# Low halves of h issued one by one, two halves of w2 cast by VectorE, a half of w1 by GpSimd

## The chip, the cores and the metric

One core of one Trainium2 chip. The metric is the device time of one execution in microseconds (us); the time before is the median of three runs, 408.17 us (408.06 to 408.4). The program text calls the engines V (VectorE, DVE in the profile), A (ScalarE, ACT), P (GpSimd, POOL), T (TensorE, PE) and SY (SyncE, SP, which here only issues DMAs).

## The reference

The output is the sum of two branches on inputs of 2048 tokens by 448 channels (the listing leaves out the shapes and the spectral branch's name for its weight):

```python
def _A_ref(x, w_r, w_i):                       # branch A: a filter in the frequency domain
    X = jnp.fft.rfft2(x, axes=(-2, -1)) * (w_r + 1j * w_i)
    return jnp.fft.irfft2(X, s=(S, D), axes=(-2, -1))
def _B_ref(x, w1, w2, w3, w4):                 # branch B
    h = _gelu(_layernorm(x, axis=-1) @ w1)
    # the four quarters of h's channels are moved by +1, -1, +2, -2 tokens -> hs
    x1 = x + hs @ w2
    return x1 + _gelu(_layernorm(x1, axis=-1) @ w3) @ w4
```

The change lies in the first 50 us of branch B, up to the product with w2.

## The kernel before

**Tiles.** The tokens are 16 blocks of 128, in four groups of four (`GRP`); token block b of a group is one half of a tile `xt`. Every product is made with numbers split into two 16-bit halves: a high half (the value rounded to float16) and a low half (value minus high half). So a matrix product takes three passes (high by high, low by high, high by low), 11 matmuls of 128x448 for one block of tokens.

**Stages around the change.** `norm1(g)` takes the layernorm statistics of a group (BN_STATS, BN_AGGR, L306 and L307), a first guess of the inverse root (L324 to L328), and normalises the four blocks in place (L333 on ACT, L336 on DVE or POOL). `powers` (L255) makes a power-of-two scale for a weight matrix from its sum of squares. `split_w` (L274) splits a weight: in the form with `low is P`, POOL scales the source in place (L276), ACT writes the high half (L277) and POOL the low half (L278); in the other form ACT writes the scaled high half (L280) and DVE the low half (L281). The four row tiles of w1 are split at L884, the last two in the POOL form, and the four of w2 at L923, all in the POOL form.

`T1(g)` transposes a normalised group on PE (L389, banks `pta`), ACT writes the high half of the transpose (L393) and DVE the low half (L394). `w1_in` (L420) is the product with w1. `w1_unit(g, i)` finishes block i of group g: gelu on ACT (L459), the high half of h on ACT (L460), and **two** low halves on DVE, one after the other (L462, k = 0 and 1; 224 columns each). The writes place the four quarters of h's channels in four different slots of `x2mem`, which is how the tokens are shifted: k = 0 writes into the slots of the two blocks behind (c-2 and c-1), k = 1 into those of the two blocks ahead (c+1 and c+2). When a block's slot has all its quarters (`DONE`), SP issues a DMA transpose of it into `hT` (L470, `h<-x2mem` in the profile). `w2_tile(b)` (L474) multiplies the block by w2 (11 matmuls L478), and DVE adds the product, scaled, into `xt` (L479).

The tile w2p holds the four high halves (slots 0 to 3) and the low halves (slots 7 to 10); two DMA copies (L924 and L925) put the high halves on the other partitions into slots 3 to 6. `load_w3([3])` and `load_w4(8, 6)` (L223, L238) are loads from HBM that SP issues behind the last DMA transpose of the first group. `turn(3)` (L854) makes the transposes of group 3 by DMA (L863, `xT<-x`), not on PE.

**Order.** A scheduler orders each engine's instructions by priorities in program order. `behind(key)` pins instructions: they are issued after the instruction that is filed under the key in `after` (`("n", 2)`: group 2's last normalisation on DVE, `("na", 2)` that on ACT, `("np", 2)` that on POOL; `("w1", t)`, `("w2", t)`: the split of a tile; `("h", g, i)`: a DMA transpose; `("r1",)`, `("e1",)`: the start and the end of w1's scale on DVE). SP issues DMAs in its order; each queue of an engine works in its order.

Of the kernel before, what the change touches and what calls it, by code (L numbers as in the profile page):

```python
# [15 lines left out]
AF = mybir.ActivationFunctionType  # L16
ALU = mybir.AluOpType
# [108 lines left out]
def body(tc, nc, x, wf, w1, w2, w3, w4, c_g, c_n, c_small, out):  # L126
    V, A, P, T, SY = nc.vector, nc.scalar, nc.gpsimd, nc.tensor, nc.sync
# [28 lines left out]
    def bank(tag, name):  # L156
        return ps.tile([128, 512], F32, tag=tag, bufs=2, name=name)
# [10 lines left out]
    def xb(b):  # L168
        return xt[b // 2][:, b % 2]
# [7 lines left out]
    def stage(name, n, side, dtype=F32):  # L177
        t = pw.tile([128, 1808], F32, tag=f"stage{side}", bufs=1, name=name)
        return (t if dtype is F32 else t.bitcast(dtype))[:, :n]
# [24 lines left out]
    w1s = stage("w1s", F, 0).rearrange("p (t n) -> p t n", t=4)  # L204
    w2s = stage("w2s", F, 1).rearrange("p (t n) -> p t n", t=4)
# [65 lines left out]
    def absmax(out_, in_):  # L271
        V.tensor_reduce(out=out_, in_=in_, axis=AX.X, op=ALU.max, apply_absolute_value=True)

    def split_w(hi, lo, src, s, low=None):  # L274
        if low is P:
            after["ps"] = (P.tensor_scalar(out=src, in0=src, scalar1=s, scalar2=0.0, op0=ALU.mult, op1=ALU.add).ins,)  # L276
            i = A.activation(out=hi, in_=src, func=AF.Copy)  # L277
            j = P.tensor_tensor(out=lo, in0=src, in1=hi, op=ALU.subtract)  # L278
            return i.ins, j.ins
        i = A.activation(out=hi, in_=src, func=AF.Copy, scale=s)  # L280
        j = V.scalar_tensor_tensor(out=lo, in0=src, scalar=s, in1=hi, op0=ALU.mult, op1=ALU.subtract)  # L281
        return i.ins, j.ins

# [35 lines left out]
    def norm1(g, apply, pins=None):  # L319

        bs, c = GRP[g], slice(4 * g, 4 * g + 4)
        mv, a, y, nm = mva[:, c], va[:, :, c], vy[:, :, c], nma[:, c]
        stats([xb(b) for b in bs], f"a{g}", mv, pins)
        V.tensor_scalar(out=a[:, 1], in0=mv[:, :, 1], scalar1=1.0 + EPS, scalar2=EPS * EPS, op0=ALU.mult, op1=ALU.add)  # L324
        V.tensor_scalar(out=a[:, 0], in0=mv[:, :, 1], scalar1=EPS, scalar2=None, op0=ALU.add)
        V.tensor_single_scalar(vyi[:, :, c], va.bitcast(I32)[:, :, c], 1, op=ALU.logical_shift_right)
        V.tensor_scalar(out=vyi[:, :, c], in0=vyi[:, :, c], scalar1=-1, scalar2=0x5F3759DF, op0=ALU.mult, op1=ALU.add)
        i = V.scalar_tensor_tensor(out=nm, in0=mv[:, :, 0], scalar=-1.0, in1=y[:, 1], op0=ALU.mult, op1=ALU.mult)  # L328
        after["c", g] = (i.ins,)
        for k, b in enumerate(bs):  # L330
            y_, m_ = y[:, 1, k:k + 1], nm[:, k:k + 1]
            if apply[k] is A:
                i = A.activation(out=xb(b), in_=xb(b), func=AF.Identity, scale=y_, bias=m_)  # L333
                after["na", g] = (i.ins,)
            else:
                i = apply[k].tensor_scalar(out=xb(b), in0=xb(b), scalar1=y_, scalar2=m_, op0=ALU.mult, op1=ALU.add)  # L336
                after["n" if apply[k] is V else "np", g] = (i.ins,)

        q, z = (pc.tile([128, 2, 4], F32, tag=f"v{t}", bufs=2, name=f"v{t}{g}") for t in "qz")
        w, r = vw[:, :, c], vr[:, :, c]  # L340

        def refine():
            P.tensor_tensor(out=q, in0=y, in1=y, op=ALU.mult)
            P.tensor_tensor(out=q, in0=q, in1=a, op=ALU.mult)
            P.tensor_scalar(out=w, in0=q, scalar1=-10.0 / 3.0, scalar2=None, op0=ALU.add)
            P.tensor_tensor(out=w, in0=w, in1=q, op=ALU.mult)
            P.tensor_scalar(out=w, in0=w, scalar1=5.0, scalar2=None, op0=ALU.add)
            P.tensor_tensor(out=z, in0=w, in1=w, op=ALU.mult)
            P.tensor_tensor(out=z, in0=z, in1=q, op=ALU.mult)
            P.tensor_scalar(out=z, in0=z, scalar1=-0.5 * 0.375 ** 3, scalar2=1.5 * 0.375, op0=ALU.mult, op1=ALU.add)  # L350
            P.tensor_tensor(out=r, in0=z, in1=w, op=ALU.mult)
            i = P.tensor_scalar(out=gsc[:, c], in0=r[:, 1], scalar1=r1, scalar2=None, op0=ALU.mult)
            after["g", g] = (i.ins,)
        return refine
# [17 lines left out]
    after = {}  # L372

    @contextlib.contextmanager
    def behind(*key):
        key = key if len(key) > 1 else key[0]
        with contextlib.ExitStack() as st:
            for i in after[key]:
                st.enter_context(tc.issue_after(i))
            yield  # L380
# [26 lines left out]
    w1p = p1.tile([128, 8, D], F16, name="w1p")  # L407
    w2p = pr.tile([128, 11, D], F16, name="w2p")
# [5 lines left out]
    def w1_in(g, units, ts, passes=range(3)):  # L414
        for p in passes:
            for t in ts:
                for i, pm in units:
                    wi, xi = ((0, 0), (0, 4), (4, 0))[p]
                    if t < 3 or p != 1:
                        m = T.matmul(pm[:, :D], xTs[g][:, xi + t, 128 * i:128 * i + 128], w1p[:, wi + t],  # L420
                                     start=t == 0 and p == 0, stop=t == 3 and p == 2)
        after["u"] = (m.ins,)
# [25 lines left out]
        for b, k in ((-2, slice(224, 448)), (-1, slice(336, 448))):  # L448
            P.tensor_copy(out=slot(b)[:, :, k], in_=slot(b - 2)[:, :, k])

    def w1_unit(g, i, pm=None):
        if pm is None:
            pm = bank(("tr" if g == 1 else "mm", "acc")[i // 2], f"pw1_{g}{i}")
            w1_in(g, [(i, pm)], range(4))
        c = CS[GRP[g][i]]
        pm = pm[:, :D]
        pv_ = pm.rearrange("p (i j n) -> p i j n", i=2, j=2)
        h = [slots_of((GRP[g][i] + 2) % NB - 2, k) for k in range(2)]
        A.activation(out=pm, in_=pm, func=AF.Gelu_apprx_tanh, scale=gsc[:, c:c + 1])  # L459
        u = A.activation(out=h[0], in_=pv_, func=AF.Copy, scale=h1)  # L460
        for k in range(2):
            v = V.scalar_tensor_tensor(out=h[1][:, k], in0=pv_[:, k], scalar=h1, in1=h[0][:, k],  # L462
                                       op0=ALU.mult, op1=ALU.subtract)
        after[g, i] = u.ins, v.ins
        for b in DONE.get(GRP[g][i], ()):
            if b == 14:
                wrap_back()
            if b // 4 not in hT:
                hT[b // 4] = pr.tile([128, 7, 512], F16, tag="h", bufs=2, name=f"h{b // 4}")
            d = SY.dma_start_transpose(out=hT[b // 4][:, :, 128 * (b % 4):128 * (b % 4) + 128],  # L470
                                       in_=slot(b if b < 14 else b - 16).rearrange("p i n -> p (i n)"))
            after["h", g, i] = (d.ins,)

    def w2_tile(b):  # L474
        pm = bank("sp", f"pw2_{b}")
# [400 lines left out]
    n1 = [norm1(0, [P,V,P,V])]  # L876
    with behind("n", 0):
        s1, r1 = powers(m1, 4, "1", "mm")
    first = [bank("mm" if k < 2 else "sp", f"pw1_0{k}") for k in range(4)]
    for t in range(4):  # L880
        with behind("p1"):
            T1(0, [t])
        with behind("a0", t):
            after["w1", t] = split_w(w1p[:, t], w1p[:, 4 + t], w1s[:, t], s1, P if t > 1 else V)  # L884
    h1 = pc.tile([128, 1], F32, name="h1")
    V.tensor_scalar(out=h1, in0=s1, scalar1=2.0 ** -5, scalar2=None, op0=ALU.mult)
    for t in range(2):
        w1_in(0, list(enumerate(first)), [t])
    n = 2
    for unit in list(enumerate(first))[:n]:  # L890
        w1_in(0, [unit], [2, 3])
    with behind("ps"):
        n1[0]()
    n1.append(norm1(1, [P, V, A, V], [("r1",), ("a0", 0), ("w1", 0), ("w1", 1)]))
    with behind("w1", 3):
        squares(m2, flat(w2s))
    T1(1)
    with behind("T", "a1"):
        for unit in list(enumerate(first))[n:2]:
            w1_in(0, [unit], [2, 3])  # L900
    with behind("n", 1), behind("u"):
        s2, r2 = powers(m2, 1, "2", first[0][:, 448:512])
    with behind("p2"):
        for unit in list(enumerate(first))[2:]:
            w1_in(0, [unit], [2, 3])
    s12 = pc.tile([128, 4], F32, name="s12")
    V.tensor_tensor(out=s12[:, 0:1], in0=h1, in1=s2, op=ALU.mult)
    V.scalar_tensor_tensor(out=s12[:, 1:2], in0=r1, scalar=2.0 ** 5, in1=r2, op0=ALU.mult, op1=ALU.mult)
# [5 lines left out]
    with behind("a1"):  # L914
        n1.append(norm1(2, [P, V, A, P], [("e2",), ("e2",), ("e2",), ("e2",)]))
    with behind("a1"), behind("n", 2):
        for k in range(2, 4):
            w1_unit(0, k, first[k])
    wrap_on()
    with behind("g", 1), behind("na", 2):  # L920
        for k in range(4):
            r = slice(0, 128 if k < 3 else 64)
            after["w2", k] = split_w(w2p[r, k], w2p[r, 7 + k], w2s[r, k], s2[r], P)  # L923
        SY.dma_start(w2p[64:128, 3:7], w2p[0:64, 0:4])  # L924
        SY.dma_start(w2p[0:64, 4:7], w2p[64:128, 0:3])  # L925
    with behind("w2", 3):
        P.memset(pairs[0][0:1], 0.0)
        P.memset(pairs[2], 0.0)
    for k in range(4):
        w1_unit(1, k)  # L930
    T1(2)
    with behind("h", 1, 3):
        load_w3([3])
# [3 lines left out]
    with behind("a2"):  # L937
        n1 = [norm1(3, [P, P, P, P])]
# [169 lines left out]
```

## Time and profile before

| | |
|---|---|
| median of 3 runs | 408.17 us (408.06 to 408.4) |
| the profiled execution's own time | 408.05 us |
| its span in the trace | 406.3 us |
| granted TensorE clock | 0.998 |
| PE busy | 399.9 us, 98% of the span |
| DVE busy | 333.6 us, 82% |
| ACT busy | 255.1 us, 63% |
| POOL busy | 100.4 us, 25% |
| moved by DMA | 52.07 MB, mean 128 GB/s |

Times in the trace count from the start of the span. A row of the timeline gives start, busy time, engine, line, operation, tiles (out<-in), shapes and, in brackets, idle time before it with the event that ended it. Between the own time and the span lie 1.75 us that the trace does not cover.

### The profile page before, as it was taken

What the parts mean: (1) busy time and instruction counts of PE and PEld (TensorE: products, weight loads), DVE (VectorE), ACT (ScalarE), POOL (GpSimd) and SP (SyncE); (2) the same over time, 40 slices, a digit from 0 to 9 for tenths busy, and PEclk for the clock granted to TensorE, in tenths of its full rate; (3) what the DMA queues carried; (4) which work ended last, traced back from release to release, by engine and by line L of the source; (5) the groups of instructions that cost most, each with busy time, mean ns of one, the idle gap of its engine ahead of it and who ended that gap; (6) DMA issues with size and microseconds to landing.
All of it is one profiled execution on the core that took longest, in us unless ns stands there. A gap on an engine that the chain in (4) does not pass through costs nothing.

```text
span 406.3 us, 8732 instructions
## 1 busy us (share of the span) xinstructions
PE 399.9 (98%) x3391; PEld 297.2 (73%) x3391; DVE 333.6 (82%) x702; ACT 255.1 (63%) x433; POOL 100.4 (25%) x158
## 2 busy tenths in 40 slices
PE   8999999999999999999999999999999999999996
PEld 3555555865667877777878878777677779998995
DVE  5898799898947887988698888965999999965645
ACT  4788889874568857655698878853354544353431
POOL 6859910111146946500021111110000000000000
PEclk9999999999999999999999999999999999999999
DMA  8978975567489661637256556510011023100101
GB/s 280 389 272 160 249 152 138 122 121 163 95 225 266 234 191 46 219 95 185 72 144 164 162 142 161 139 27 2 24 69 70 24 90 92 47 2 2 45 2 45
DMA packets 54596, 52.07 MB, mean 128 GB/s; under 512 B 35678, under 2 KB 48542, under 8 KB 54556
## 3 DMA queue, kind: packets, MB, share of 16 engines
q1 hardware_dynamic: 54556, 51.53, 46.0%
q8 instruction: 26, 0.43, 0.4%
q14 instruction: 14, 0.11, 0.1%
HBM read 38.28 MB, written 3.67 MB: 103 GB/s over the span
## 4 chain that ended last, share of the span: by engine, by line
PE 87%; POOL 5%; DMA 2%; DVE 2%; ACT 2%; issue 1%; SPq 0%; POOLq 0%; ACTq 0%
PE pw L400 33%; PE acc L808 23%; PE pw L478 6%; PE side L778 4%; PE acc L778 3%; PE pu L667 3%; PE ps L567 3%; PE pe L688 2%; PE pp L622 2%; PE px L639 2%; PE py L709 2%; PE pw L420 2%; DMA w1s<-w 1%; POOL xt L336 1%; DMA h<-x2mem 1%
## 5 line engine op out<-in xcount | busy, mean ns | idle before, releaser
L400 PE MATMUL pw<-x2mem,w3p 128*128 128x256 f16 x1232 | 151.3, 273 | 0.0
L400 PEld LDWEIGHTS <-w3p 128*128 128x128 f16 x1232 | 118.9, 98 | 19.3
L808 PE MATMUL acc<-w4p,hf 128*128 128x448 f16 (+1 forms) x516 | 104.4, 348 | 0.0
L808 PEld LDWEIGHTS <-hf 128*128 128x128 f16 x516 | 50.1, 98 | 37.6
L726 ACT ACTIVATE pw<-pw,pe 128x512 f32<-128x512 f32 x42 | 27.4, 654 | 26.8 <-PE pw L400 26.6
L729 DVE SCALAR_TENSOR_TENSOR hf<-pw,h,hf 128x512 f16<-128x512 f32 x42 | 31.3, 746 | 12.9 <-ACT hf L728 12.7
L478 PE MATMUL pw<-w2p,h 128*128 128x448 f16 x176 | 35.8, 353 | 0.9 <-DMA h<-x2mem 0.9
L420 PE MATMUL pw<-w1p,xT 128*128 128x448 f16 x176 | 34.9, 352 | 0.1
L648 POOL TENSOR_TENSOR z<-te 128x450 f32<-128x450 f32 x16 | 15.7, 983 | 70.8 <-DVE te L646 65.9
L728 ACT ACTIVATE hf<-pw,h 128x512 f16<-128x512 f32 x42 | 28.9, 687 | 5.0 <-PE acc L808 4.0
L478 PEld LDWEIGHTS <-h 128*128 128x128 f16 x176 | 17.0, 98 | 17.0 <-DMA h<-x2mem 2.0
L744 ACT ACTIVATE hz<-g,h 128x896 f16<-128x896 f32 x14 | 14.6, 1044 | 23.1 <-DVE g L741 23.1
L420 PEld LDWEIGHTS <-xT 128*128 128x128 f16 x176 | 17.1, 99 | 16.1 <-DVE xT L394 0.4
L778 PEld LDWEIGHTS <-hz 128*128 128x128 f16 x294 | 28.3, 98 | 0.6
L629 ACT ACTIVATE pf<-pp 64x450 f16<-64x450 f32 x32 | 17.4, 544 | 12.5 <-DVE pf L630 9.7
L630 DVE TENSOR_TENSOR pf<-pp,pf 64x450 f16<-64x450 f32 x32 | 19.9, 622 | 5.1 <-ACT pf L629 4.7
L745 DVE SCALAR_TENSOR_TENSOR hz<-g,h,hz 128x896 f16<-128x896 f32 x14 | 16.1, 1148 | 6.8 <-ACT hz L744 6.8
L550 POOL TENSOR_TENSOR f<-xr 128x452 f32<-128x452 f32 x16 | 19.7, 1251 | 0.6
L558 DVE TENSOR_TENSOR xh<-f,xh 128x452 f16<-128x452 f32 x16 | 14.3, 916 | 5.7 <-ACT xh L557 5.7
L644 ACT ACTIVATE te<-px 64x450 f32<-64x450 f32 x32 | 17.3, 541 | 1.2 <-PE px L639 0.6
L738 ACT ACTIVATE g<-pw,pe 128x512 f32<-128x512 f32 x14 | 9.6, 683 | 11.3 <-PE pw L400 11.3
L547 POOL TENSOR_TENSOR xr<-xf 128x452 f32<-128x452 f32 x8 | 9.2, 1156 | 22.3 <-issue 16.4
(188 smaller groups left out, 705.7 us busy)
## 6 DMA issues: line engine op xcount, KB each, us to landing
wc<-wf SPq DMA_DIRECT2D x32, 225.0 KB, 3.7
wl<-wf SPq DMA_DIRECT2D x8, 450.0 KB, 4.3
xt<-x SPq DMA_DIRECT2D x8, 448.0 KB, 7.1
xf<-x SPq DMA_DIRECT2D x8, 448.0 KB, 4.6
loads<-x SPq DMA_DIRECT2D x7, 448.0 KB, 4.0
out<-xt SPq DMA_DIRECT2D x13, 224.0 KB, 1.9
w3raw<-w SPq DMA_DIRECT2D x3, 896.0 KB, 10.8
gn<-c_g SPq DMA_DIRECT2D x16, 128.0 KB, 3.0
```

The costliest lines, as they stand in the source:

```text
L400: T.matmul(ps_out, wp[:, wi + t, cols], xT[:, xi + t, tok], start=t == 0 and wi + xi == 0, stop=t == 3 and wi == 4)
L420: m = T.matmul(pm[:, :D], xTs[g][:, xi + t, 128 * i:128 * i + 128], w1p[:, wi + t], start=t == 0 and p == 0, stop=t == 3 and p == 2)
L478: T.matmul(pm[:, :D], h[:, k], w2p[:, w], start=n == 0, stop=n == 10)
L550: P.tensor_tensor(out=f[:, :, k:k + 2].rearrange("p b s d -> p s b d"), in0=u[:, :, 0], in1=u[:, :, 1], op=op)
L629: A.activation(out=hi, in_=src, func=AF.Copy)
L630: V.tensor_tensor(out=lo, in0=src, in1=hi, op=ALU.subtract)
L644: A.activation(out=e[64 * h:64 * h + 64], in_=px_[64 - 64 * h:128 - 64 * h, :2 * DF], func=AF.Copy)
L726: A.activation(out=pm, in_=pm, func=AF.Gelu_apprx_tanh, scale=r3)
L728: i = A.activation(out=h[:, 0], in_=pm, func=AF.Copy, scale=h3)
L729: j = V.scalar_tensor_tensor(out=h[:, 1], in0=pm, scalar=h3, in1=h[:, 0], op0=ALU.mult, op1=ALU.subtract)
L778: m = T.matmul(to, h[:, hi, 128 * blk:128 * blk + 128], b[wi], start=new and n == 0, stop=n == 2 and (last if blk in (2, 5, 3, 0) else end ...
L808: m = T.matmul(to, h[:, hi, o:o + 128], w4p[0][:, wi, f, r], start=first and f % 2 == 0 and n == 0, stop=end and f % 2 == 1 and n == 2, sk ...
```

## The change

1. `split_w` can have its high half made by POOL. The high half of w1's first tile moves from ACT to POOL (L281 of the new text).
2. In group 1's `norm1`, the first block's statistic is pinned behind `e1` (the end of w1's scale on DVE) and no longer behind `r1` (its start).
3. `w1_unit` takes the low halves to issue (`ks`) and returns a function that issues a single one. The halves are issued in an order written by hand, those that the first DMA transposes need first.
4. The scaling of w2 (POOL, L930) is written apart from the split. The high halves of tiles 0 and 1 stay on ACT (L935), those of tiles 2 and 3 become `tensor_copy` on DVE (L934, CAST in the profile), and POOL subtracts (L939).
5. The two DMA copies inside w2p are pinned behind the DMA transpose `("h", 1, 0)`; SP now issues the smaller one first.

```diff
-    def split_w(hi, lo, src, s, low=None):
+    def split_w(hi, lo, src, s, low=None, high=None):
...
-        i = A.activation(out=hi, in_=src, func=AF.Copy, scale=s)
+        if high is P:
+            i = P.tensor_scalar(out=hi, in0=src, scalar1=s, scalar2=0.0, op0=ALU.mult, op1=ALU.add)
+        else:
+            i = A.activation(out=hi, in_=src, func=AF.Copy, scale=s)
...
-    def w1_unit(g, i, pm=None):
+    def w1_unit(g, i, pm=None, ks=range(2)):
...
-        for k in range(2):
+
+        def low(k):
             v = V.scalar_tensor_tensor(out=h[1][:, k], in0=pv_[:, k], scalar=h1, in1=h[0][:, k],
                                        op0=ALU.mult, op1=ALU.subtract)
-        after[g, i] = u.ins, v.ins
+            after[g, i] = u.ins, v.ins
+
+        for k in ks:
+            low(k)
...
+        return low
...
-            after["w1", t] = split_w(w1p[:, t], w1p[:, 4 + t], w1s[:, t], s1, P if t > 1 else V)
+            after["w1", t] = split_w(w1p[:, t], w1p[:, 4 + t], w1s[:, t], s1, (V, V, P, P)[t], P if t in (0,) else A)
...
-    n1.append(norm1(1, [P, V, A, V], [("r1",), ("a0", 0), ("w1", 0), ("w1", 1)]))
+    n1.append(norm1(1, [P, V, A, V], [("e1",), ("a0", 0), ("w1", 0), ("w1", 1)]))
...
     with behind("a1"), behind("n", 2):
-        for k in range(2, 4):
-            w1_unit(0, k, first[k])
+        lows = {(0, k): w1_unit(0, k, first[k], ()) for k in range(2, 4)}
+        lows[0, 3](0)
     wrap_on()
-    with behind("g", 1), behind("na", 2):
+    r = [slice(0, 128)] * 3 + [slice(0, 64)]
+    with behind("g", 1):
         for k in range(4):
-            r = slice(0, 128 if k < 3 else 64)
-            after["w2", k] = split_w(w2p[r, k], w2p[r, 7 + k], w2s[r, k], s2[r], P)
+            P.tensor_scalar(out=w2s[r[k], k], in0=w2s[r[k], k], scalar1=s2[r[k]], scalar2=0.0, op0=ALU.mult, op1=ALU.add)
+
+    def w2_hi(k, e):
+        if e is V:
+            return V.tensor_copy(out=w2p[r[k], k], in_=w2s[r[k], k]).ins
+        return A.activation(out=w2p[r[k], k], in_=w2s[r[k], k], func=AF.Copy).ins
+
+    def w2_lo(k):
+        with behind("np", 2):
+            after["w2", k] = (P.tensor_tensor(out=w2p[r[k], 7 + k], in0=w2s[r[k], k], in1=w2p[r[k], k], op=ALU.subtract).ins,)
+
+    w2_hi(0, A)
+    w2_lo(0)
+    lows[1, 0] = w1_unit(1, 0, None, (0,))
+    with behind("n", 2):
+        lows[0, 2](1)
+    lows[1, 1] = w1_unit(1, 1, None, (0,))
+    with behind("n", 2):
+        for unit, k in (((0, 3), 1), ((1, 0), 1), ((0, 2), 0)):
+            lows[unit](k)
+    with behind("na", 2):
+        w2_hi(1, A)
+    w2_lo(1)
+    with behind("n", 2):
+        w2_hi(2, V)
+    w2_lo(2)
+    with behind("n", 2):
+        w2_hi(3, V)
+    w2_lo(3)
+    with behind("h", 1, 0):
         SY.dma_start(w2p[64:128, 3:7], w2p[0:64, 0:4])
         SY.dma_start(w2p[0:64, 4:7], w2p[64:128, 0:3])
...
-    for k in range(4):
-        w1_unit(1, k)
+    lows[1, 2] = w1_unit(1, 2, None, (0,))
+    lows[1, 1](1)
+    lows[1, 3] = w1_unit(1, 3, None, (0,))
+    for k in range(2, 4):
+        lows[1, k](1)
     T1(2)
```

How the engines' orders move. **VectorE**, from the first low half of block (1, 0) (`pw_10`, the product of group 1, block 0) to the first low half of the transposes of group 2 (`xT_509`). Before:

```order
L462 SCALAR_TENSOR_TENSOR x2mem<-pw_10_440,h_252,x2mem 128x2x112 x2
L327 TENSOR_SCALAR vy<-vy 128x2x4
L328 SCALAR_TENSOR_TENSOR nma<-mva,vy 128x4
L336 TENSOR_SCALAR xt_79<-xt_79,vy,nma 128x448
L462 SCALAR_TENSOR_TENSOR x2mem<-pw_02_211,h_252,x2mem 128x2x112 x2
L462 SCALAR_TENSOR_TENSOR x2mem<-pw_03_212,h_252,x2mem 128x2x112 x2
L462 SCALAR_TENSOR_TENSOR x2mem<-pw_11_458,h_252,x2mem 128x2x112 x2
L394 TENSOR_TENSOR xT_509<-pta_510,xT_509 128x512
```

The same place on VectorE after the change:

```order
L467 SCALAR_TENSOR_TENSOR x2mem<-pw_10_427,h_252,x2mem 128x2x112
L330 TENSOR_SCALAR vy<-vy 128x2x4
L331 SCALAR_TENSOR_TENSOR nma<-mva,vy 128x4
L339 TENSOR_SCALAR xt_79<-xt_79,vy,nma 128x448
L467 SCALAR_TENSOR_TENSOR x2mem<-pw_03_212,h_252,x2mem 128x2x112
L467 SCALAR_TENSOR_TENSOR x2mem<-pw_02_211,h_252,x2mem 128x2x112
L467 SCALAR_TENSOR_TENSOR x2mem<-pw_03_212,h_252,x2mem 128x2x112
L467 SCALAR_TENSOR_TENSOR x2mem<-pw_10_427,h_252,x2mem 128x2x112
L467 SCALAR_TENSOR_TENSOR x2mem<-pw_02_211,h_252,x2mem 128x2x112
L934 CAST w2p<-w2s 128x448
L934 CAST w2p<-w2s 64x448
L467 SCALAR_TENSOR_TENSOR x2mem<-pw_11_445,h_252,x2mem 128x2x112 x2
```

One low half stands ahead of `vy` where there were two, and the two casts stand between the low halves of group 0 and those of block (1, 1).

**SyncE**, from the first transpose of h's group 0 (`h_456`) to that of the next blocks (`h_598`). Before:

```order
L470 DMA_TRANSPOSE h_456<-x2mem 128x7x128
L924 DMA w2p<-w2p 64x1792
L925 DMA w2p<-w2p 64x1344
L470 DMA_TRANSPOSE h_456<-x2mem 128x7x128 x3
L223 DMA w3raw<-w 64x1792 x2
L238 DMA w4half<-w 128x6x448
L863 DMA_TRANSPOSE xT_720<-x_721 128x7x128
L470 DMA_TRANSPOSE h_598<-x2mem 128x7x128
L863 DMA_TRANSPOSE xT_720<-x_721 128x7x128 x2
```

The same place on SyncE after the change:

```order
L478 DMA_TRANSPOSE h_442<-x2mem 128x7x128
L961 DMA w2p<-w2p 64x1344
L960 DMA w2p<-w2p 64x1792
L478 DMA_TRANSPOSE h_442<-x2mem 128x7x128 x3
L223 DMA w3raw<-w 64x1792 x2
L238 DMA w4half<-w 128x6x448
L872 DMA_TRANSPOSE xT_720<-x_721 128x7x128 x2
L478 DMA_TRANSPOSE h_598<-x2mem 128x7x128
L872 DMA_TRANSPOSE xT_720<-x_721 128x7x128 x2
```

The copies have changed places, and the first transpose of `h_598` (for token block 4) now stands behind two transposes of `xT_720`, where one stood ahead of it.

**GpSimd**, from the normalisation of group 0 to the second low half of w1. Before:

```order
L336 TENSOR_SCALAR xt_76<-xt_76,vy,nma 128x448
L276 TENSOR_SCALAR w1s<-w1s,pe_205 128x448 x2
L343 TENSOR_TENSOR vq_198<-vy 128x8
L344 TENSOR_TENSOR vq_198<-vq_198,va 128x8
L345 TENSOR_SCALAR vw<-vq_198 128x2x4
L346 TENSOR_TENSOR vw<-vw,vq_198 128x2x4
L347 TENSOR_SCALAR vw<-vw 128x2x4
L348 TENSOR_TENSOR vz_199<-vw 128x8
L349 TENSOR_TENSOR vz_199<-vz_199,vq_198 128x8
L278 TENSOR_TENSOR w1p<-w1s,w1p 128x448
```

The same place on GpSimd after the change:

```order
L339 TENSOR_SCALAR xt_76<-xt_76,vy,nma 128x448
L281 TENSOR_SCALAR w1p<-w1s,pe_205 128x448
L276 TENSOR_SCALAR w1s<-w1s,pe_205 128x448 x2
L346 TENSOR_TENSOR vq_198<-vy 128x8
L347 TENSOR_TENSOR vq_198<-vq_198,va 128x8
L348 TENSOR_SCALAR vw<-vq_198 128x2x4
L349 TENSOR_TENSOR vw<-vw,vq_198 128x2x4
L278 TENSOR_TENSOR w1p<-w1s,w1p 128x448
```

POOL makes w1's first high half ahead of its scalings, and the first low half (L278) comes after four small operations of the refinement where it came after seven.

More of the change, by code (lines that the diff above doesn't have):

```diff
@@ L888, in body @@
         w1_in(0, list(enumerate(first)), [t])
-    n = 2
-    for unit in list(enumerate(first))[:n]:
-        w1_in(0, [unit], [2, 3])
+    units = list(enumerate(first))
+    w1_in(0, [units[0]], [2, 3])
+    w1_in(0, [units[1]], [2, 3])
     with behind("ps"):
         n1[0]()
-    n1.append(norm1(1, [P, V, A, V], [("r1",), ("a0", 0), ("w1", 0), ("w1", 1)]))
+    n1.append(norm1(1, [P, V, A, V], [("e1",), ("a0", 0), ("w1", 0), ("w1", 1)]))
     with behind("w1", 3):
@@ L897, in body @@
     T1(1)
-    with behind("T", "a1"):
-        for unit in list(enumerate(first))[n:2]:
-            w1_in(0, [unit], [2, 3])
     with behind("n", 1), behind("u"):
@@ L903, in body @@
     with behind("p2"):
-        for unit in list(enumerate(first))[2:]:
-            w1_in(0, [unit], [2, 3])
+        w1_in(0, [units[2]], [2, 3])
+    with behind("p2"):
+        w1_in(0, [units[3]], [2, 3])
     s12 = pc.tile([128, 4], F32, name="s12")
```

## The prediction

> **What bounds the kernel now.** I read the page first: the share of each engine, then what TensorE waited for, then TensorE's timeline at those waits.
>
> ```profile
> PE 399.9 (98%) x3391; PEld 297.2 (73%) x3391; DVE 333.6 (82%) x702; ACT 255.1 (63%) x433; POOL 100.4 (25%) x158
> ```
>
> TensorE is busy for 399.9 of 406.3 us, and the change takes no matmul away. So it can only win what TensorE idles, 6.4 us at most. The waits of TensorE, all of them:
>
> ```profile
> PE wps L838 <- DVE wsrc L192: 1.2, 1, 1.2
> PE pw L478 <- DMA h<-x2mem: 0.9, 3, 0.4
> PE pta L389 <- POOL xt L336: 0.7, 1, 0.7
> PE pm L260 <- DVE pt L258: 0.4, 1, 0.4
> ```
>
> The first is the start of the warm-up and stays. The second and third lie in the stage that the change edits. The timeline of TensorE shows where:
>
> ```profile
> 13.80 4.84 PE L420 MATMUL pw<-w1p,xT 128*128 128x448 f16 x23
> 19.30 1.97 PE L389 MATMUL pta<-ident,xt 128*128 128x128 f32 x16 [0.66 <-POOL xt L336]
> 21.24 10.37 PE L420 MATMUL pw<-w1p,xT 128*128 128x448 f16 x54
> 31.45 1.91 PE L389 MATMUL pta<-ident,xt 128*128 128x128 f32 x16
> 33.72 1.31 PE L478 MATMUL pw<-w2p,h 128*128 128x448 f16 x6 [0.36 <-DMA h<-x2mem]
> 37.39 2.26 PE L478 MATMUL pw<-w2p,h 128*128 128x448 f16 x11 [0.28 <-DMA h<-x2mem]
> 39.48 7.35 PE L420 MATMUL pw<-w1p,xT 128*128 128x448 f16 x38
> 46.67 4.33 PE L478 MATMUL pw<-w2p,h 128*128 128x448 f16 x22
> 51.21 2.25 PE L478 MATMUL pw<-w2p,h 128*128 128x448 f16 x11 [0.22 <-DMA h<-x2mem]
> ```
>
> A matmul's drawn end overlaps the next one, so the time that a wait truly costs is the distance of two starts beyond the usual pitch, 0.19 us (7.35 us for 38). By that measure the wait at 19.30 costs 0.82 us, that at 33.72 costs 0.52, that at 37.39 costs 0.44 and that at 51.21 costs 0.38; the row at 13.80 holds another 0.23 us (23 matmuls need 4.5, it has 4.84 with its tail). Together 2.4 us. Behind 51.21 TensorE goes on in one row after the other; what starts there later or earlier shifts the end by as much. **So the question is one number: when does the product with block 4 start, 51.21 us before?** It starts when its DMA transpose has landed. The issues on SP's queue:
>
> ```profile
> 30.68 1.34 SPq L470 DMA_TRANSPOSE h<-x2mem  x1
> 32.13 0.53 SPq L924 DMA_DIRECT2D w2p<-w2p  x1
> 32.71 0.59 SPq L925 DMA_DIRECT2D w2p<-w2p  x1
> 33.39 4.36 SPq L470 DMA_TRANSPOSE h<-x2mem  x3
> 37.80 1.22 SPq L223 DMA_DIRECT2D w3raw<-w  x2
> 39.07 0.59 SPq L238 DMA_DIRECT2D w4half<-w  x1
> 44.65 1.82 SPq L863 DMA_TRANSPOSE xT<-x  x1
> 46.57 1.83 SPq L470 DMA_TRANSPOSE h<-x2mem  x1
> 48.51 2.85 SPq L863 DMA_TRANSPOSE xT<-x  x2
> ```
>
> The issues with the time to landing (the list of DMA issues cut to the moment of one issue; the rows in the order of 30.68, 39.07, 44.65, 46.57 and 48.51):
>
> ```profile
> h<-x2mem SPq DMA_TRANSPOSE x1, 3.0
> w4half<-w SPq DMA_DIRECT2D x1, 1344.0 KB, 10.6
> xT<-x SPq DMA_TRANSPOSE x1, 5.8
> h<-x2mem SPq DMA_TRANSPOSE x1, 4.6
> xT<-x SPq DMA_TRANSPOSE x1, 3.5
> ```
>
> A transpose lands 3.0 us after its issue when it is alone. Here they land at 39.07 + 10.6 = 49.6 (w4half), 44.65 + 5.8 = 50.4, 46.57 + 4.6 = 51.2 and 48.51 + 3.5 = 52.0: one after the other, 0.79 us apart, behind the w4 load. Block 4's transpose at 51.17 is thus set by three things: when the w4 load ends, and how many transposes stand between.
>
> **The change part by part.** *Order of the low halves.* The rows on VectorE:
>
> ```profile
> 27.28 0.17 DVE L324 TENSOR_SCALAR va<-mva 128x4 f32<-128x4 f32 x1
> 27.91 0.81 DVE L462 SCALAR_TENSOR_TENSOR x2mem<-pw,h,x2mem 128x224 f16<-128x224 f32 x2 [0.19 <-ACT x2mem L460]
> 29.03 0.51 DVE L336 TENSOR_SCALAR xt<-xt,vy,nma 128x448 f32<-128x448 f32 x1
> 29.46 2.24 DVE L462 SCALAR_TENSOR_TENSOR x2mem<-pw,h,x2mem 128x224 f16<-128x224 f32 x6
> ```
>
> A low half follows the last at 0.36 us (2.24 for six). The first transpose was issued at 30.68, behind the fourth of the six; now it needs the first two after the normalisation, and one half in front of that is gone: 3 x 0.36 = 1.07 earlier, issue at 29.6 and landing at 32.6, before TensorE's transposes end. The wait at 33.72 goes (-0.52).
>
> *Two casts on VectorE.* No cast of this shape stands in the trace. The nearest row is the 128x448 normalisation, 0.51 us; above it, POOL's 1.04 us (rows below) if a lock is waited for. They stand ahead of block (1, 1)'s low halves, and these release the second transpose (33.39). VectorE's fifth half ends at 30.9; without a wait casts and two halves end by 32.7, the second transpose is issued at about 33.0, the fourth at 35.9 and the w3 load at 37.2, not 37.80: 0.6 earlier. The wait at 37.39 goes (-0.44). If I take the casts for nothing, SP gains 1.0 at most; if each waits a whole POOL operation, it loses 0.4.
>
> *POOL beside VectorE.* Rows of POOL, and one of VectorE:
>
> ```profile
> 10.82 1.25 POOL L276 TENSOR_SCALAR w1s<-w1s,pe 128x448 f32<-128x448 f32 x2 [0.83 <-DMA w1s<-w]
> 14.07 0.73 POOL L348 TENSOR_TENSOR vz<-vw 128x8 f32<-128x8 f32 x1
> 14.88 0.20 POOL L349 TENSOR_TENSOR vz<-vz,vq 128x8 f32<-128x8 f32 x1
> 16.45 1.03 POOL L278 TENSOR_TENSOR w1p<-w1s,w1p 128x448 f16<-128x448 f32 x1
> 30.96 1.04 POOL L278 TENSOR_TENSOR w2p<-w2s,w2p 128x448 f16<-128x448 f32 x1
> 16.92 0.58 DVE L324 TENSOR_SCALAR va<-mva 128x4 f32<-128x4 f32 x1
> 14.09 0.66 DVE L281 SCALAR_TENSOR_TENSOR w1p<-w1s,pe,w1p 128x448 f16<-128x448 f32 x1
> ```
>
> Here the two engines block each other. VectorE's tiny operation at 16.92 takes 0.58 us where its twin at 27.28 takes 0.17, and ends as POOL's subtraction ends (16.45 + 1.03 = 17.48). POOL's tiny one at 14.07 takes 0.73 and not 0.20, and ends as VectorE's low half of w1 ends (14.75). The Trainium skill, "SBUF — State Buffer", section "Who interferes with whom", states why: the two share a port pair, a VectorE cast or scaling holds it whole, and whoever comes first blocks the other fully. It speaks against this change, which puts two such casts beside POOL's four subtractions; the rows above agree with it.
>
> So cast 2 (ready at 30.9) meets POOL's first subtraction, which starts at about 30.4 (POOL is about 0.5 earlier) and ends at 31.5. It waits 0.6, ends near 31.7, and cast 3 follows directly, before POOL has its next subtraction, which needs no more than a turn of 0.05 us: this is the thinnest point, and I take the better end. That wait is in the 33.0 above.
>
> *w1's first high half on POOL and the statistic.* POOL gets one more operation of 0.62 (1.25 for two) and starts 0.17 earlier, since VectorE's 0.62 us statistic no longer stands in w1's scale. So POOL's chain to the normalised block that TensorE waits for at 19.30 is 0.45 longer. Against this, POOL's first low half stands three operations earlier in order, and a blocked operation such as 14.07 (0.5 lost) may go. I call s the shift of the transposes at 19.30. It lies between 0.45 - 0.53 - 0.4 (a second blocked one) = -0.45 and 0.45 + 0.15 = +0.6; as far as the rows say, it is a tie who comes first, VectorE's low half of w1's second tile or POOL's subtraction (both near 14.1). I take s = +0.25. The 0.23 us at 13.80 are in s: that gap precedes the wait at 19.30, and closing it alone gains nothing, since POOL's block still decides.
>
> *What is late next.* Stage by stage, TensorE now reaches the products with blocks 2 and 3 (46.67) 0.96 - s earlier, about 45.9. They need the scale `cs` that POOL works out at 45.16; POOL is about 0.5 earlier, so a wait of up to 0.3 may open. It costs nothing, since the next wait is longer: TensorE is ready for block 4 at about 50.2, but its transpose comes now **behind two** transposes of xT (order of SyncE), one more than before.
>
> The sum for that start: the w4 load lands 0.6 earlier (49.0), one more transpose ahead of block 4 costs 0.79, and all of group 1 comes s = 0.25 later: -0.6 + 0.79 + 0.25 = +0.44. What was gained at 33.72 and 37.39 is given back at 51.21, where TensorE then waits about 1.4 us and not 0.38. The profiled execution would take 408.05 + 0.45 = 408.5 us; the median of the runs lies 0.12 above the profiled one, so **408.6 us**. Bounds: s from -0.45 to +0.6 and the w4 load from 1.0 earlier to 0.4 later give -0.66 to +1.79, that is 407.5 to 410.0.
>
> **The rivals.** *One: faster.* The pace of 0.79 us might be the tail of the w4 load and not the price of a transpose; then block 4's transpose lands 3.0 after its issue. That is about 47.3 (two issues of 1.8 behind a first one at 44), so 50.3, and the product starts when VectorE has freed the bank (51.10 before; 0.7 earlier with the scale, 50.4). With s = 0 this is 0.8 earlier: 407.4 us, and with the best s 406.9. For it: between 49.6 and 52.0 the load is only just over. Against it: three landings at one distance, with issues 1.9 apart.
>
> *Two: slower.* Cast 3 loses the port to POOL's second subtraction. The point that decides is whether it starts before POOL's next operation at about 31.5 to 31.75. If it loses, it waits 1.04 us, block (1, 1)'s low halves, the second transpose, both loads and block 4 move by 1.0 us: +1.44 in all, 409.6 us. (By the rule of the Trainium skill's page named above, "SBUF — State Buffer", it would go this way whenever POOL's subtraction has started first, and the sum would be 409.6; by the row of 0.51 us alone it is 408.6.) For it: the rows at 14.07 and 16.92. Against it: VectorE's two casts are adjacent, and POOL has a small operation to pass in between.
>
> *Three: nothing.* If the w4 load ends 0.8 earlier and s is 0, block 4 comes at 51.2 as before: 408.2 us. This is the middle of the range between the forecast and the first rival.
>
> **How the numbers follow.** Forecast (+0.1 to +0.8) 0.45; nothing (-0.8 to +0.1) 0.13; faster 0.15; slower by the lock, or with s = 0.6 and a late load, 0.27. A measurement of this kernel can tell about 0.2%, 0.8 us, from no change. Faster by more than that: 0.15. Within: 0.55, the forecast nearly whole and the third. Slower: 0.30, the second with the top of the forecast. Eight in ten: from 407.4, where part of the first rival is left out, to 409.7, which takes in the second.
>
> **What would show it.** In the new profile: the h transposes first issued near 29.6 and no wait of TensorE near 33 and 37; VectorE's casts at 0.5 us, or one near 1.0 with an end that falls on a POOL row; a low half of w1 or a POOL row of over 1.2 us near 14; the wait for block 4 as the largest in TensorE's list, about 1.4 us, with three landings 0.8 apart. I am wrong if block 4's transpose lands without the second xT transpose's 0.8, or if a wait opens behind 52 us, where I count none.

## The result and the profile after

| | before | after |
|---|---|---|
| median | 408.27 us (407.95 to 408.81, 8 runs) | 409.37 us (408.88 to 409.84, 8 runs) |
| ratio | | 1.0026, 95% interval 1.0017 to 1.0034 |
| profiled execution, its span | 408.05, 406.3 us | 409.39, 407.6 us |
| start of group 1's transposes on TensorE | 19.30 | 20.02 |
| first product with block 4 | 51.21 | 52.27 |
| last matmul | 402.75 | 403.79 |

The change made the kernel slower by 1.1 us, 0.26%. The forecast was 408.6, in a range of 407.4 to 409.7; by the bound of 0.2% the result lies just on the slower side.

What TensorE waits for after the change, all of it (engine, line, what it waited for: us in total, times, the longest):

```profile
PE wps L847 <- DVE wsrc L192: 1.2, 1, 1.2
PE pw L423 <- DVE xT L397: 0.6, 1, 0.6
PE pw L487 <- DMA h<-x2mem: 0.6, 1, 0.6
PE pw L487 <- DVE xt L488: 0.5, 1, 0.5
PE pta L392 <- POOL xt L339: 0.5, 1, 0.5
```

Two of these are new, that on VectorE's `xT` and that on VectorE's `xt`; the waits for h transposes have shrunk from three to one. The timeline of TensorE at those places:

```profile
17.81 1.69 PE L423 MATMUL pw<-w1p,xT 128*128 128x448 f16 x8 [0.62 <-DVE xT L397]
20.02 1.97 PE L392 MATMUL pta<-ident,xt 128*128 128x128 f32 x16 [0.52 <-POOL xt L339]
...
36.76 3.06 PE L487 MATMUL pw<-w2p,h 128*128 128x448 f16 x14
...
47.36 4.32 PE L487 MATMUL pw<-w2p,h 128*128 128x448 f16 x22 [0.55 <-DVE xt L488]
52.27 2.25 PE L487 MATMUL pw<-w2p,h 128*128 128x448 f16 x11 [0.59 <-DMA h<-x2mem]
```

The wait near 33.7 is gone and that near 37.4 is down to about 0.2 (it lies inside the row at 36.76); 0.72 us is lost at 20.02, and by the distance of starts 0.71 at 47.36 and 0.76 at 52.27. From 52.27 on every matmul that both kernels issue in the same order comes 1.04 to 1.06 us later, down to the last one: what the change does is complete with the first product of block 4, and nothing is won or lost behind it.

VectorE and POOL, where the two low halves of w1 meet:

```profile
12.42 0.97 DVE L284 SCALAR_TENSOR_TENSOR w1p<-w1s,pe,w1p 128x448 f16<-128x448 f32 x1
14.44 1.40 DVE L284 SCALAR_TENSOR_TENSOR w1p<-w1s,pe,w1p 128x448 f16<-128x448 f32 x1
```

```profile
14.32 1.04 POOL L278 TENSOR_TENSOR w1p<-w1s,w1p 128x448 f16<-128x448 f32 x1
```

VectorE's low half of w1's second tile took 0.66 us before and takes 1.40: POOL's subtraction started 0.12 us ahead of it, ended at 15.36, and VectorE's operation ends 0.48 us behind that (15.84). The same 0.48 us lie between the two ends in experiments 2, 6 and 12. Everything behind it on VectorE, the transposes' low halves and the statistics of group 1, comes later, and TensorE's waits at 17.81 and 20.02 follow.

SP's issues:

```profile
30.28 1.34 SPq L478 DMA_TRANSPOSE h<-x2mem  x1
32.45 0.53 SPq L961 DMA_DIRECT2D w2p<-w2p  x1
33.07 0.55 SPq L960 DMA_DIRECT2D w2p<-w2p  x1
33.71 4.35 SPq L478 DMA_TRANSPOSE h<-x2mem  x3
38.12 1.22 SPq L223 DMA_DIRECT2D w3raw<-w  x2
39.38 0.59 SPq L238 DMA_DIRECT2D w4half<-w  x1
43.87 4.78 SPq L872 DMA_TRANSPOSE xT<-x  x2
48.75 1.53 SPq L478 DMA_TRANSPOSE h<-x2mem  x1
```

Their time to landing (the list of DMA issues, cut to the issues at 43.87, 45.91 and 48.75):

```profile
xT<-x SPq DMA_TRANSPOSE x1, 6.8
xT<-x SPq DMA_TRANSPOSE x1, 5.5
h<-x2mem SPq DMA_TRANSPOSE x1, 3.5
```

The w4 load lands at 49.88, and the transposes at 50.65, 51.43 and 52.23: again one after the other, 0.78 us apart, with block 4's in third place.

### The profile page after: what moved, and what is told of

It reads as the page before. It is cut to its first block, busy times and chain, and to the rows that moved or that the text cites. A ratio compares the mean times of both kernels' runs of the same rounds, so it can differ in the third digit from the quotient of the medians.

```text
span 407.6 us, 8731 instructions
## 1 busy us (share of the span) xinstructions
PE 400.4 (98%) x3391; PEld 297.6 (73%) x3391; DVE 335.4 (82%) x704; ACT 253.7 (62%) x430; POOL 101.5 (25%) x159
## 4 chain that ended last, share of the span: by engine, by line
PE 89%; POOL 4%; DVE 2%; DMA 2%; ACT 1%; issue 1%; SPq 0%; DVEq 0%
PE pw L403 33%; PE acc L817 23%; PE pw L487 6%; PE side L787 4%; PE acc L787 3%; PE pu L676 3%; PE ps L576 3%; PE pe L697 2%; PE pp L631 2%; PE px L648 2%; PE py L718 2%; PE wps L847 2%; PE pw L423 2%; POOL xt L339 1%; POOL w2p L939 1%; DMA h<-x2mem 1%
```

## The experiments

**Theory A**: three shifts add up at block 4's transpose: what POOL and VectorE lose ahead of 20 us (+0.72 in the profile), the second xT transpose (+0.79), less what the low halves' order wins on SP (-0.46). **Theory B**: the queue of DMAs alone counts, a shift at 20 us is absorbed behind the w4 load. **Theory C**: the order of the DMA transposes is hidden, the loss at 20 us is all. Medians belong to 6 to 12 runs beside 21 to 31 of the kernel before, whose median lay between 408.07 and 408.22; the trace's times come from one execution each. The first data come in at slightly different times, so that the scale's matmul of w1 (the first `pm`, L260) starts at 9.5 to 10.2; stages are therefore compared by distances.

The medians need one more caution. An execution's own time exceeds its span by 1.65 to 1.83 us in every run of the kernel before, of the changed kernel and of most experiments, but by a median of 1.9 us in experiment 6, 2.1 in 7 and 2.2 in 12. The trace does not cover that part, and its cause is open. So for these three the median span stands beside the median: it is 406.4 to 406.5 before, 407.6 for the changed kernel, 406.7 in 6, 405.85 in 7, 405.95 in 8 and 406.1 in 12.

| kernel | ratio to before | median | `pm` to group 1's transposes | these to block 4's product |
|---|---|---|---|---|
| before | | 408.07 to 408.27 | 9.75 | 31.92 |
| changed | 1.0026 (1.0017 to 1.0034) | 409.37 | 10.42 | 32.26 |
| 1: w1's half on ACT | 1.0031 (1.0019 to 1.0042) | 409.30 | 9.90 | 32.14 |
| 2: one xT transpose ahead | 1.0009 (0.9999 to 1.0019) | 408.62 | 10.05 | 31.59 |
| 3: both | 1.0007 (0.9996 to 1.0017) | 408.32 | 9.56 | 31.63 |
| 4: before, two xT ahead | 1.0020 (1.0011 to 1.0029) | 408.95 | 9.58 | 32.67 |
| 5: as 1 | 1.0031 (1.0020 to 1.0042) | 409.57 | 9.85 | 32.20 |
| 6: before, w1's half on POOL | 1.0009 (0.9999 to 1.0019) | 408.59 | 9.92 | 31.86 |
| 7: before, `cs` first | 0.9995 (0.9986 to 1.0005) | 407.92 | 10.37 | 31.28 |
| 8: as 1, `cs` first | 0.9987 (0.9979 to 0.9996) | 407.75 | 9.87 | 30.80 |
| 9, 10: as 1 | one run each | 409.69, 409.43 | 9.83, 9.64 | 32.25, 32.26 |
| 11: as 8, casts on ACT | 1.0010 (1.0001 to 1.0019) | 408.45 | 9.83 | other order |
| 12: changed, `cs` first | 1.0005 (0.9996 to 1.0014) | 408.27 | 10.05 | 30.60 |

### 1 to 3: each of the two losses undone, and both

```diff
 1: in the changed kernel
-(V, V, P, P)[t], P if t in (0,) else A)
+(V, V, P, P)[t], A)
 2: in the changed kernel, turn()
-            d = SY.dma_start_transpose(out=xTs[g][:, :, 128 * i:128 * i + 128], in_=h)
+            with behind("h", 2, 0) if i else contextlib.nullcontext():
+                d = SY.dma_start_transpose(out=xTs[g][:, :, 128 * i:128 * i + 128], in_=h)
 3: both
```

> The changed kernel with w1's first high half made by ACT again; all else as changed. Theory A (the shifts add up: 0.72 us of port lock ahead of the transposes at 20.02, then 0.8 us for a second xT transpose ahead of block 4's, less 0.45 that SP gains): VectorE's low half of w1's second tile takes about 0.7 us and not 1.40, TensorE's transposes of group 1 start at 19.3 to 19.5 and not 20.02, block 4's product at 51.5 to 51.7 and not 52.27, the time is 0.6 to 0.7 us below the changed kernel, about 408.7. Theory B (only the queue of DMAs counts; a shift at 20 us is absorbed behind the w4 load): the transposes start earlier, but block 4's product stays at 52.2 and the time at 409.4. Theory C (only the waits before 21 us carry through, the order of the DMA transposes is hidden): as A.

> The changed kernel with one xT transpose ahead of block 4's h transpose, as before the change. Theory A: block 4's transpose lands at 51.4 and not 52.23; the product then waits for VectorE to free the bank (51.60 in the changed kernel), starts near 51.65, and the time falls by 0.6 us, to about 408.8. Theory B: lands 0.8 earlier, the same fall. Theory C (the order is hidden): no fall of over 0.2, 409.3.

> Both of the edits above. Theory A: the two add up; block 4's product starts near 51.0, the time is about 1.2 to 1.3 us below the changed kernel, 408.1, as before the change or 0.2 better. Theory B: as the second edit alone, 408.8. Theory C: as the first alone, 408.7.

In the first, the lock is gone and the transposes start earlier; VectorE's low half (first row, experiment 1) against that of the second experiment (second fence, with POOL's row):

```profile
14.24 0.65 DVE L284 SCALAR_TENSOR_TENSOR w1p<-w1s,pe,w1p 128x448 f16<-128x448 f32 x1
```

```profile
14.22 1.41 DVE L284 SCALAR_TENSOR_TENSOR w1p<-w1s,pe,w1p 128x448 f16<-128x448 f32 x1
```

```profile
14.11 1.04 POOL L278 TENSOR_TENSOR w1p<-w1s,w1p 128x448 f16<-128x448 f32 x1
```

The same instruction takes 0.65 us where POOL's is not ahead of it and 1.41 where POOL's started 0.11 earlier. In the first experiment the transposes of group 1 start at 19.51, block 4's product at 51.65 and the last matmul at 403.27, 0.52 earlier than in the changed kernel, as theory A has it; theory B's 52.2 is wrong. But the median did not move (409.30): this half of theory A's expectation failed, and experiments 5, 9 and 10 look for the reason.

The second did what theory A said: block 4's transpose lands at 51.04 and no longer at 52.23, and the median falls by 0.75 us. TensorE's row:

```profile
47.10 6.53 PE L487 MATMUL pw<-w2p,h 128*128 128x448 f16 x33 [0.68 <-DVE xt L488]
```

The 33 matmuls of blocks 2, 3 and 4 are one row, with 0.13 us of wait in it; the wait that is left is ahead of it, for VectorE's `xt` and through it for POOL's `cs`. Theory C, which had no fall of over 0.2 us, is refuted. The third lies 0.30 us below the second (0.48 by the traces at 103 us, 0.28 at the last matmul), less than the 0.6 to 0.7 that theory A expected; the runs of either kernel spread over some 1.5 us, so the 0.30 by itself is not clear of noise.

### 4: one more xT transpose, and nothing else

```diff
 before: block 4's DMA (unit 2, 0) is held back, in turn(3):
+            with behind("h", 2, 0) if i > 1 else contextlib.nullcontext():
                 d = SY.dma_start_transpose(out=xTs[g][:, :, 128 * i:128 * i + 128], in_=h)
+            if i == 1:
+                after["two"] = (d.ins,)
+                with behind("two"):
+                    held.pop()()
```

> The kernel before with a single difference: block 4's h transpose is issued behind two xT transposes and not one. Theories A and B: its landing moves from 51.17 to 51.96 and the time rises by 0.8 us, to 409.0. Theory C: no change that can be told, 408.3.

TensorE's waits in the profile of this kernel, and its row at block 4:

```profile
PE pw L484 <- DMA h<-x2mem: 1.6, 3, 1.1
```

```profile
52.00 2.25 PE L484 MATMUL pw<-w2p,h 128*128 128x448 f16 x11 [1.08 <-DMA h<-x2mem]
```

It landed at 51.96 and not 51.17, the product started 0.79 us later, and the median rose by 0.73 us, ratio 1.0020. A place in the queue of DMA transposes costs TensorE its 0.79 us in full where TensorE waits for it. Theory C is refuted again.

### 5, 9 and 10: why the first kernel's time did not fall

> The changed kernel with w1's first high half on ACT, once more: in the first run the trace had its last matmul 0.52 us earlier than the changed kernel's, but the time was the same (409.3). Theory A (the shifts add up): the trace is what counts; the last matmul again 0.5 to 0.7 us earlier and the time 408.6 to 408.9. Theory B (a shift at 20 us is absorbed): 409.3.

> The changed kernel with w1's first high half on ACT, a third look, since the two medians (409.30, 409.57) lie 0.7 to 1.0 us above what their profiled executions' matmuls say. Theory A: the profiled execution has its first product with block 4 some 32.2 us behind the transposes of group 1, as the two before, and the excess lies outside this stage. Theory B (a shift at 20 us is absorbed at block 4): an execution with a later landing shows up, 32.7 or more behind them.

> The same kernel, a fourth look, with the same expectations: theory A, 32.2 us from the transposes of group 1 to block 4's product; theory B, 32.7 or more in some execution.

In all four profiled executions of this kernel the stage is as theory A has it: 9.64 to 9.90 and 32.14 to 32.26 us in the table's two last columns, the last matmul 0.22 to 0.69 us earlier than in the changed kernel. The difference in the profiles lies at the very end. The last store of the output (the list of DMA issues, cut to that issue): the changed kernel, then experiments 1, 5, 9 and 10:

```profile
out<-xt SPq DMA_DIRECT2D x1, 112.0 KB, 1.7
```

```profile
out<-xt SPq DMA_DIRECT2D x1, 112.0 KB, 2.8
```

```profile
out<-xt SPq DMA_DIRECT2D x1, 112.0 KB, 1.8
```

```profile
out<-xt SPq DMA_DIRECT2D x1, 112.0 KB, 2.8
```

```profile
out<-xt SPq DMA_DIRECT2D x1, 112.0 KB, 2.8
```

In three of four executions it lands 1.0 us later, and nowhere else: the last landing is 2.5 to 2.7 us behind the last matmul's start in the profiles of the ten other kernels and in experiment 5, and 3.5 to 3.6 in experiments 1, 9 and 10. Experiment 5's profiled execution, without it, was the fastest of its 8 runs (408.90; the others 409.18 to 409.83). So in these four executions the matmuls' gain, 0.2 to 0.7 us, was there, and in three of them a late last landing covers it. That the runs without a profile went the same way is likely, but not shown. Theory B's later landing at block 4 did not show up. Why this kernel's last store lands late more often is open; its issue, its data and the work around it are the same.

### 6: w1's half on POOL, by itself

```diff
 before: split_w with high=, as in the change, and
-            after["w1", t] = split_w(w1p[:, t], w1p[:, 4 + t], w1s[:, t], s1, P if t > 1 else V)
+            after["w1", t] = split_w(w1p[:, t], w1p[:, 4 + t], w1s[:, t], s1, (V, V, P, P)[t], P if t in (0,) else A)
-    n1.append(norm1(1, [P, V, A, V], [("r1",), ("a0", 0), ("w1", 0), ("w1", 1)]))
+    n1.append(norm1(1, [P, V, A, V], [("e1",), ("a0", 0), ("w1", 0), ("w1", 1)]))
```

> The kernel before with two small edits alone: w1's first high half on POOL, and the statistic behind the end of w1's scale. Theory A: POOL's subtraction comes to stand where VectorE's low half of w1's second tile is ready, that low half takes 1.2 to 1.4 us and not 0.66, the transposes of group 1 start near 20.0 and not 19.30, block 4's product at 51.8 and not 51.21, and the time rises by 0.5 to 0.7 us, to 408.8. Theory B: transposes later, block 4's product and the time as before, 408.2.

```profile
14.62 1.12 DVE L284 SCALAR_TENSOR_TENSOR w1p<-w1s,pe,w1p 128x448 f16<-128x448 f32 x1
```

The low half took 1.12 us beside POOL's subtraction (14.23 to 15.26), the transposes started at 19.91, block 4's product at 51.77 and the last matmul at 403.29, and the median rose by 0.52 us. That is theory A's lower bound, but 0.2 us of it lie outside the span (406.7 against 406.4), the interval of this ratio (0.9999 to 1.0019) alone does not exclude zero, and its profile measured from `pm` shows only 0.17 us.

### 7, 8 and 12: block 4's transpose first in the queue

```diff
 scales():
-        P.tensor_scalar(out=c, in0=c, scalar1=s12[:, 0:1], scalar2=None, op0=ALU.mult)
+        after["cs", g] = (P.tensor_scalar(out=c, in0=c, scalar1=s12[:, 0:1], scalar2=None, op0=ALU.mult).ins,)
 norm1(..., gate): the operations on DVE and POOL that normalise stand in
+                with behind(*gate) if gate else contextlib.nullcontext():
 group 3:
-        n1 = [norm1(3, [P, P, P, P])]
+        n1 = [norm1(3, [P, P, P, P], gate=("cs", 0))]
 7: in before; 8: in experiment 1's kernel (with 2's pin, which changes no order there); 12: in the changed kernel
```

> The kernel before with one pin more: POOL works out the scale cs ahead of the normalisation of group 3, not behind it; with that the transposes of xT come later, and block 4's h transpose is first behind the w4 load. Theories A and B (block 4's product waits for the queue): it lands near 50.4 and not 51.17, VectorE has freed the bank by then, the product starts near 50.5 and the time falls by 0.7 us, to 407.5. Theory C (the order of the transposes is hidden): no change, 408.2.

> The changed kernel with w1's first high half on ACT and POOL's scale cs ahead of the normalisation of group 3, so that block 4's h transpose is first behind the w4 load. Theory A: the gain of the new order of the low halves (the w4 load ends 0.4 us earlier than before) is no longer given back: block 4's product starts at 50.0 to 50.2, 1.0 to 1.2 us earlier than before the change; the time falls to 407.2, or to 407.7 if the filter stage near 144 us, which began to wait in the third experiment, keeps part. Theory B: about 407.8.

> The eighth experiment's kernel with w1's first high half on POOL, as in the change: with block 4 off the queue of transposes, nothing behind 21 us waits, so what POOL costs there goes through whole. Theory A: transposes of group 1 start 0.3 to 0.6 us later after the first matmul of the scale, the time is 408.1 to 408.4 (407.75 in the eighth). Theory B: absorbed, 407.75.

In experiment 8 the two waits at 47 and 52 are gone:

```profile
40.21 6.22 PE L424 MATMUL pw<-w1p,xT 128*128 128x448 f16 x32
46.26 6.41 PE L488 MATMUL pw<-w2p,h 128*128 128x448 f16 x33
52.50 0.28 PE L260 MATMUL pm<-pt,ones 128*128 128x1 f32 x2
```

The three products follow each other without a wait: block 4 starts 30.80 us behind group 1's transposes (31.92 before). That gain of 1.1 us is in part given back, for SP now issues transposes of the next stage ahead of the h transposes of later blocks:

```profile
73.85 2.25 PE L488 MATMUL pw<-w2p,h 128*128 128x448 f16 x11
...
78.23 2.06 PE L488 MATMUL pw<-w2p,h 128*128 128x448 f16 x10 [0.24 <-DMA h<-x2mem]
```

By the distances of starts 0.21 and 0.41 us are lost there. What is left is 407.75, ratio 0.9987 (0.9979 to 0.9996): this version beats both kernels, by 0.3 us the kernel before and by 1.6 the changed one.

Experiment 7's median fell by 0.15 us (407.92, expected 407.5), with an interval that includes no change. Its span fell by 0.5 us (405.85 against 406.4); the rest went outside the span. Its profile has block 4's product 0.64 earlier by the distance, and nothing is lost behind it (351.51 us from there to the last matmul, 351.54 before). In that execution everything started late, since a statistic on VectorE waited for a load; this is the 10.37 in the table:

```profile
10.55 0.63 DVE L306 BATCH_NORM_STATS2 sta<-xt 128x6 f32<-128x448 f32 x1 [0.78 <-DMA xt<-x]
```

Experiment 12 was to price w1's half where no queue hides it, and leaves the price open. Its median is 408.27 against 407.75, +0.52 us, as theory A expected, but 0.38 of that lie outside the span, and the spans differ by 0.15 (406.1 against 405.95). Its profile has the low half of w1 at 1.41 us again, yet from `pm` the transposes start only 0.18 later than in experiment 8 (0.3 to 0.6 was expected), and block 4's product no later (40.65 against 40.67).

### 11: the casts on ACT

```diff
 in experiment 8's kernel, without 2's pin
-        w2_hi(2, V)
+        w2_hi(2, A)
...
-        w2_hi(3, V)
+        w2_hi(3, A)
```

> The eighth experiment's kernel (w1's half on ACT, cs first) with the two casts of w2 on ACT too, so that VectorE has no cast between the low halves. If the casts on VectorE cost the SP queue their 1.05 us, the second h transpose is issued near 32.3 (33.3 in the eighth), the w3 load 0.7 earlier, no wait is left at 37.5 (0.23 there), and TensorE goes without a wait from 20 us to beyond 60; the time falls to 407.0 to 407.4. If the casts were free (another wait holds the second transpose), issue and time stay, 407.75.

SP's issues and TensorE's row in the profile:

```profile
30.16 1.34 SPq L479 DMA_TRANSPOSE h<-x2mem  x1
31.60 0.53 SPq L961 DMA_DIRECT2D w2p<-w2p  x1
32.22 1.40 SPq L479 DMA_TRANSPOSE h<-x2mem  x1
```

```profile
36.08 0.74 PE L488 MATMUL pw<-w2p,h 128*128 128x448 f16 x3 [1.30 <-DMA h<-x2mem]
```

The second h transpose was issued at 32.22, as expected for casts that had cost VectorE their time (12.45 us behind group 1's transposes, 13.71 in experiment 8). But the scheduler also put block 1's product ahead of product work with w1 on TensorE, where it waits 1.46 us for the landing at 36.03; the time was 408.45, not 407.0 to 407.4. By these two profiles the casts cost SP about 1.2 us there; that taking them away gains time was not shown.

## Why the prediction was nearly right

- **The bound and the place.** Right. The product with block 4 sets the end; its shift, 1.06, is the shift of the last matmul, 1.04. The waits at 33.7 and 37.4 were won (0.52 and 0.2) and given back at block 4, as forecast.
- **The second xT transpose, +0.79.** Right to the hundredth: 52.23 - 49.88 is 2.35 us for three, and experiment 4 has 0.79 for the one alone.
- **The term s, +0.25 taken, -0.45 to +0.6 allowed** (the lower sum is -0.48 as it is written). This is the term that was mis-sized. It was called a tie who comes first near 14.1, and POOL came first, by 0.12 us (14.32 against 14.44). The profile has +0.72, outside the bounds given for it. The upper bound was POOL's longer chain, 0.45, and 0.15 more, less than a block costs VectorE: 0.74 us at w1's second tile (1.40 for 0.66). In this execution the first low half was blocked too (0.97 for 0.67), since POOL's second scaling began 0.48 us late, at 12.28, just behind the landing of its load at about 12.15 (first fence below). The Trainium skill, "SBUF — State Buffer", section "Who interferes with whom", which has the earlier starter block the other in full, agrees with these rows. How much of the 0.72 belongs to every execution is open. Experiments 2 and 12 run the same program up to there and have 10.05 us from `pm` to the transposes, +0.30 on the 9.75 before and so close to the forecast; in both the first low half took 0.65. With the half on ACT the distance is 9.56 to 9.90, but for the 10.37 of experiment 7 with its late load. By the median spans the half costs 0.3 us in experiment 6 and in 2 against 3, and 0.15 in 12 against 8.
- **The w4 load, -0.6.** It landed 0.26 later; less s = 0.72 that is -0.46. Counted in the same way, the eight other profiles with the new order of the low halves and the casts on VectorE have -0.43 to -0.69, so the size was about right. The first cast waited for POOL's subtraction (0.82 us), and the low halves of block (1, 1) were as late as the forecast had it, but s moves all of them.
- **The casts.** The better end was taken and it came: 0.82 and 0.38 us, the second without a wait (second fence below). No row gave the turn of 0.05 us on which that end rested; POOL did a small operation of 0.34 us first, and the second cast, at 32.31, was ahead of its next subtraction, at 32.41. That margin is thin, though the two casts take 1.12 us together in experiments 2 and 12 as well. The lock that cost the time was the one at w1.
- **`cs`.** Wrong: it was to come 0.5 earlier and came 1.1 later (46.59, not 45.47). Before, all steps that lead to `cs` but the last stood ahead of group 3's normalisation on POOL; now they stand between and behind its four operations. Two of these took 1.09 and 1.01 us for 0.71 while VectorE's subtractions for the same group ran. That VectorE's operations held the port is argued from this overlap. So the wait at 47.36 (0.71) opened, and that for block 4 was 0.76 and not the 1.4 of the forecast; together they are about as long as that. The later `cs` cost nothing as long as block 4's transpose was later still, as forecast for a smaller wait; in experiment 2 it became the next bound, and in experiment 8 taking it away was part of the gain.
- **The sum.** 0.72 - 0.46 + 0.79 = 1.05 us, where 0.44 was forecast, with s the term that was mis-sized. That 409.37 still lies in the range is in part luck: the range reached up to 409.7 for a lock at the casts, which did not come, and the lock at w1 filled that room.

POOL's late scaling, for the point on s:

```profile
12.28 0.64 POOL L276 TENSOR_SCALAR w1s<-w1s,pe 128x448 f32<-128x448 f32 x1 [0.48 <-ACT w1p L283]
```

The row names ACT, but in experiment 2 the same scaling started ahead of that operation's end; so the load, issued at 4.75 and landed 7.4 us later, is the likely releaser. The two casts, with POOL's rows around them:

```profile
31.56 1.12 DVE L934 CAST w2p<-w2s 128x448 f16<-128x448 f32 x2
```

```profile
31.10 1.03 POOL L939 TENSOR_TENSOR w2p<-w2s,w2p 128x448 f16<-128x448 f32 x1
32.10 0.34 POOL L347 TENSOR_TENSOR vq<-vq,va 128x8 f32<-128x8 f32 x1
32.41 2.18 POOL L939 TENSOR_TENSOR w2p<-w2s,w2p 128x448 f16<-128x448 f32 x2
```

VectorE's `xt`, which releases TensorE at 47.36, in the changed kernel, for the point on `cs`:

```profile
46.62 1.27 DVE L488 SCALAR_TENSOR_TENSOR xt<-xt,cs,pw 128x448 f32<-128x448 f32 x2 [1.09 <-POOL cs L368]
```

```profile
42.44 1.78 POOL L339 TENSOR_SCALAR xt<-xt,vy,nma 128x448 f32<-128x448 f32 x2
44.39 1.01 POOL L339 TENSOR_SCALAR xt<-xt,vy,nma 128x448 f32<-128x448 f32 x1
46.27 0.32 POOL L368 TENSOR_SCALAR cs<-cs,s 128x12 f32<-128x12 f32 x1
```

## What to carry to other kernels

An early finish on one engine is worth nothing where a transfer behind a shared queue is late: read at the next wait for a transfer what stands ahead of it, and move that; one transpose was 0.79 us here. Where two engines block each other, a tie of a tenth of a microsecond is decided by who starts first, and the loser pays the other's rest and passes it to all behind it; price such a tie at its dear end. And a change of order in one place reorders other places: experiments 8 and 12 won their stage and lost 0.6 us of it 20 to 30 us later, and experiment 3 lost 0.2 near 144 us.

## What the runs showed of the hardware that was not expected

- The last store of the output landed 1.0 us later (2.8 and not 1.7 us) in three of four profiled executions of one kernel, whose matmuls were on time; in no profile of the others. Its cause is open.
- The part of the own time that the trace does not cover was 1.7 to 1.8 us in most kernels, but 1.9, 2.1 and 2.2 in experiments 6, 7 and 12, more than some of the effects measured here. Its cause is open.
- The times of first data vary between executions: the scale's first matmul started anywhere from 9.54 to 10.19 us with the same program ahead of it, more than some of the effects measured here, so single profiles are compared by distances within them.
